# Linear attention ahead of two feed-forward layers: queries and keys of chunks 8 to 23 transposed by 32x32 blocks on VectorE and through DRAM, and query-times-state on 64x64 tiles

## Chip, cores and metric

The kernel runs on one core of a Trainium2 chip. The metric is the device time of one execution in microseconds; before the change the median of three runs is 1184.46 us (1184.09 to 1187.66).

## What is computed

The input is q, k, v of 4 batches x 8 heads x 768 tokens x 64, all float32, and the float64 weights of two feed-forward layers. Attention is a decayed linear recurrence per batch and head, and its output, 3072 tokens x 512, runs through two layers of the same shape:

```python
gamma = 1.0 - 2.0 ** (-5.0 - np.arange(H))
for t in range(S):
    state = gamma * state + outer(k[t], v[t])
    y[t] = (q[t] @ state) / sqrt(D)
x = y.transpose(0, 2, 1, 3).reshape(B * S, H * D)
x = gated(x @ w_in) @ w_out        # h * sigmoid(1.702 h)
out = rational(x @ w2_in) @ w2_out # P(h) / Q(h)
```

## The kernel before

Attention works on 24 chunks of 128 tokens, six per batch. The decays are folded into q and k (`scale_chunk`, line 181): q is multiplied by growing powers of gamma, k by falling ones, on VectorE from chunk 8 on and mostly on GpSimd before. A chunk then has three parts. **T** (`att_T`, lines 198 to 209) transposes q and k with the identity on PE, eight 128x128 transposes into two PSUM banks, and copies them to qT and kT on ACT. **S** (`att_S`, line 211) forms the scores of the eight heads, two heads on the two 64-row halves of PE at a time, and multiplies them by the causal mask on VectorE into sm (line 221). **Y** (`att_Y`, line 224) adds query times state (line 231, called Z below), scores times values (line 234), and, but for the last chunk of a batch, key times value (line 242), which VectorE adds to the state `st` (line 252). `st` holds two heads as diagonal blocks of a 128x128 tile, so the query-times-state matmuls are 128x128 with half of their weights zero; a memset on GpSimd puts the zeros there. y is split into a rounded high part xh (ACT, line 246) and a low part xl (VectorE, line 247).

The layers run in 2 x 6 blocks of 512 tokens and 16 steps each. A step has 12 matmuls of the first product (`g1`, lines 294 to 296, into hp) and 12 of the second (`g2`, lines 313 to 319, into o), each 128x512; between them ACT and VectorE apply the activation (z, gh, gl; lines 367 to 374). `g1` runs two steps ahead in layer 1. VectorE and ACT also turn float64 weight words into float32 (`w_first`, `w_bits`, lines 121 to 136: operations on tiles s and u, here called conversion) and split them into high and low parts (`w_split`, line 147).

Chunks 0 to 3 are done before the first step (the head). Chunks 4 to 23 are spread over the first five blocks of layer 1: a list `todo` (lines 410 to 436) puts the T, S and Y parts of four chunks beside the first 13 steps of each block. All DMAs are issued from SyncE in program order; the other engines' order is set by a scheduler. Raw q, k, v come into a pool of six tiles, so the loads for chunk c+2 wait for chunk c. Scores, transposes and y share two PSUM banks (tag "a"); qT and kT have one buffer each.

Of the kernel before, what the change touches and what calls it, by code (L numbers as in the profile page):

```python
# [9 lines left out]
F32 = mybir.dt.float32  # L10
# [19 lines left out]
def constants():  # L30
    """Identity, causal mask and decay tables: they depend on the shapes alone."""
    gamma = 1.0 - 2.0 ** (-5.0 - np.arange(H, dtype=np.float64))
    t = np.arange(S, dtype=np.float64).reshape(NCH, P)
    up = gamma[None, None, :] ** (t[:, :, None] + 1.0) / np.sqrt(D)
    down = gamma[None, None, :] ** -(t[:, :, None] + 1.0)
    i = np.arange(P)
    c = np.concatenate(
        [
            np.eye(P),
            (i[None, :] >= i[:, None]).astype(np.float64),  # L40
            up.transpose(1, 0, 2).reshape(P, NCH * H),
            down.transpose(1, 0, 2).reshape(P, NCH * H),
        ],
        axis=1,
    )
    return np.ascontiguousarray(c.astype(np.float32))
# [3 lines left out]
def tile_kernel(ctx: ExitStack, tc: tile.TileContext, q, k, v, w1i, w1o, w2i, w2o, pa, pb, cst, out):  # L50
# [27 lines left out]
    # A unit is half of what a step needs: 512 columns of the input or of the output weights.  # L78
    dr_w = {}
# [83 lines left out]

# [1 line left out]
    RAW = {}  # L165
    QK = {}
    SM = {}
    X = {}

    def load_raw(c, nm, pool=None, tag="raw"):  # L170
        b, cc = divmod(c, NCH)
        src = {"q": q, "k": k, "v": v}[nm]
        t = (pool or at).tile([P, H, D], F32, tag=tag, name=f"raw{nm}{c}")
        nc.sync.dma_start(out=t, in_=src[b, :, cc * P : (cc + 1) * P, :].rearrange("h p d -> p h d"))
        RAW.setdefault(c, []).append(t)

# [4 lines left out]
    def scale_chunk(c):  # L181
        cc = c % NCH
        for nm, t in zip("qk", RAW[c]):
            f = tab[nm][:, cc, :].unsqueeze(2).to_broadcast([P, H, D])
            eng = nc.vector if c >= 8 or (c < 4 and nm == "q") else nc.gpsimd
            eng.tensor_tensor(out=t, in0=t, in1=f, op=ALU.mult)
# [10 lines left out]

    def att_T1(c, n, tag, alt=None):
        nm = "qk"[n]
        pt = ps(tag, f"pT{nm}{c}")  # L200
        for p in range(NP):
            nc.tensor.transpose(pt[:, p, :], RAW[c][n][:, 2 * p : 2 * p + 2, :].rearrange("p h d -> p (h d)"), ident)
        t = at_tile(c, nm + "T", alt)
        nc.scalar.copy(out=t, in_=pt)
        QK.setdefault(c, []).append(t)

    def att_T(c, tg, alt=None):
        for n in range(2):
            att_T1(c, n, tg[n], alt)

    def att_S(c, tg, alt=None):
        qT, kT = QK[c]
        pss = [ps(tg[n], f"pS{n}_{c}") for n in range(2)]
        for p in range(NP):
            for n in range(2):
                r = slice(64 * n, 64 * n + 64)
                nc.tensor.matmul(pss[n][:, p, :], kT[r, p, :], qT[r, p, :], start=(p == 0), stop=True, skip_group_check=True)  # L217
        SM[c] = []
        for n in range(2):
            t = at_tile(c, f"sm{n}", alt)  # L220
            nc.vector.tensor_tensor(out=t, in0=pss[n], in1=mask, op=ALU.mult)
            SM[c].append(t)

    def att_Y(c, tg, xh, xl, o):
        b, cc = divmod(c, NCH)
        kr, vr = RAW[c][1:]
        qT = QK[c][0]
# [4 lines left out]
        for p in range(NP):  # L232
            for n in range(2):
                nc.tensor.matmul(  # L234
                    py[64 * n : 64 * n + 64, p, :], vr[:, 2 * p + n, :], SM[c][n][:, p, :],
                    start=(p == 0 and cc == 0), stop=True, skip_group_check=True,
                )
        if cc < NCH - 1:
            pk = ps(tg[1], f"pK{c}")
            for p in range(NP):  # L240
                for n in range(2):
                    nc.tensor.matmul(
                        pk[64 * n : 64 * n + 64, p, 0:D], kr[:, 2 * p + n, :], vr[:, 2 * p + n, :],
                        start=(p == 0), stop=True, skip_group_check=True,
                    )
        nc.scalar.copy(out=xh[:, :, o : o + P], in_=py)
        nc.vector.tensor_tensor(out=xl[:, :, o : o + P], in0=py, in1=xh[:, :, o : o + P].bitcast(F32), op=ALU.subtract)  # L247
        if cc < NCH - 1:
            for n in range(2):
                r = slice(64 * n, 64 * n + 64)  # L250
                if cc:
                    nc.vector.tensor_tensor(out=st[r, :, r], in0=pk[r, :, 0:D], in1=st[r, :, r], op=ALU.add)
                else:
                    nc.vector.tensor_copy(out=st[r, :, r], in_=pk[r, :, 0:D])

# [1 line left out]
    blocks = {1: [4] * 6, 2: [4] * 6}  # L257
    steps = []
# [62 lines left out]
    def evac(layer, bi, t0, n):  # L321
# [11 lines left out]
        for d in range(0, n // P, 2):  # L333
            t = ws.tile([P, 2, DM], F32, tag="s", name=f"os{layer}_{bi}_{d}")
            for x in range(2):
                if last and x:
                    nc.vector.tensor_copy(out=t[:, x, :], in_=acc[d + x])
                else:
                    nc.scalar.copy(out=t[:, x, :], in_=acc[d + x])
                if last:  # L340
                    nc.sync.dma_start(out=out[t0 + (d + x) * P : t0 + (d + x + 1) * P, :], in_=t[:, x, :])
# [66 lines left out]

# [60 lines left out]
    with tc.manual_schedule(engines={mybir.EngineType.SP}):  # L469
# [25 lines left out]
        keep_warm(10)  # L495
        nc.gpsimd.memset(st, 0.0)
        x_tiles(1, 0, blocks[1][0] * P)
# [10 lines left out]

        scale_chunk(0)
        att_T1(0, 0, "a")  # L510
        keep_warm(2)
        att_T1(0, 1, "a")
        keep_warm(2)
        scale_chunk(1)
        att_T1(1, 0, "a", "gh")
        keep_warm(5)
        att_T1(1, 1, "a", "gh")
        S(0)
# [24 lines left out]
        for i in range(-lead[1], NS):  # L543
# [80 lines left out]
```

## Time and profile before

| what | value |
|---|---|
| median of 3 runs | 1184.46 us |
| lowest, highest | 1184.09, 1187.66 us |
| span of the profiled execution (first to last instruction) | 1183.0 us |
| granted TensorE clock, mean of the span | 0.997 |
| PE busy | 1168.6 us, 99% |
| VectorE (DVE) busy | 845.7 us, 71% |
| ScalarE (ACT) busy | 610.4 us, 52% |
| GpSimd (POOL) busy | 15.6 us |

The profiled execution's own time is not listed apart from its span; the runs lie 1.1 to 4.7 us above the span. Busy times are sums over the engine's instructions. Matmuls overlap in the pipeline, so the distance from the start of one to the start of the next tells what it costs, not its own duration.

### The profile page before, as it was taken

The page shows a single profiled execution, that of the slowest core. Times are in us where ns is not written, and L with a number is a line of the kernel's source. Part 1 is how long each engine was busy: PE and PEld are TensorE (multiplying, and loading weights), DVE is VectorE, ACT ScalarE, POOL GpSimd, SP SyncE. Part 2 cuts the span into 40 slices and gives each one's busy share as a digit, 9 for nine tenths or more (in the row PEclk, how much of TensorE's full clock was granted, in tenths as well). Part 3 has the DMA queues.
Part 4 walks back from the last instruction along what each step waited for, and adds up shares of the span by engine and source line. Part 5 has one row for each costly group of instructions (what it writes and reads, how often), then busy time and mean ns, then how long its engine had stood idle before and what let it go on. Part 6 is the DMA issues. An engine that isn't in the chain of part 4 may idle for free.

```text
span 1183.0 us, 15510 instructions
## 1 busy us (share of the span) xinstructions
PE 1168.6 (99%) x6067; PEld 962.7 (81%) x6067; DVE 845.7 (71%) x1372; ACT 610.4 (52%) x1030; POOL 15.6 (1%) x17
## 2 busy tenths in 40 slices
PE   8899999999999999999999999999999999999998
PEld 5787888888888888888888888888888888888887
DVE  6999945545464554553455898888988988988886
ACT  3555523232233323332344876866766766866765
POOL 1100000000000000000000000000000000000000
PEclk9999999999999999999999999999999999999999
DMA  9944233343342423440343200200200200200000
GB/s 255 308 123 114 63 110 88 89 128 86 81 125 77 126 83 101 122 134 1 115 122 109 73 18 1 72 1 1 72 1 1 71 1 1 71 1 1 36 1 36
DMA packets 128600, 89.26 MB, mean 75 GB/s; under 512 B 78224, under 2 KB 111120, under 8 KB 128528
## 3 DMA queue, kind: packets, MB, share of 16 engines
q1 hardware_dynamic: 128528, 88.28, 25.9%
q8 instruction: 47, 0.77, 0.3%
q14 instruction: 25, 0.20, 0.1%
HBM read 67.29 MB, written 20.97 MB: 75 GB/s over the span
## 4 chain that ended last, share of the span: by engine, by line
PE 90%; DVE 8%; issue 1%; DMA 0%; ACT 0%; SPq 0%; POOL 0%
PE hp L294 14%; PE hp L296 14%; PE hp L295 14%; PE o L317 7%; PE o L319 7%; PE o L318 7%; PE o L313 7%; PE o L315 6%; PE o L314 6%; PE pS L217 2%; PE pY L234 2%; DVE u L133 2%; DVE s L135 1%; PE pY L231 1%; DVE s L131 1%; DVE u L132 1%
## 5 line engine op out<-in xcount | busy, mean ns | idle before, releaser
L294 PE MATMUL hp<-xh,wi 128*128 128x512 f32 x768 | 303.4, 395 | 4.9 <-DVE xl L247 2.7
L296 PE MATMUL hp<-xh,wi 128*128 128x512 f32 x768 | 299.7, 390 | 0.0
L295 PE MATMUL hp<-xl,wi 128*128 128x512 f32 x768 | 299.7, 390 | 0.0
L294 PEld LDWEIGHTS hp<-xh,wi 128*128 128x128 f32 x768 | 144.6, 188 | 38.1 <-DVE wi L147 4.5
L296 PEld LDWEIGHTS hp<-xh,wi 128*128 128x128 f32 x768 | 144.6, 188 | 30.7
L295 PEld LDWEIGHTS hp<-xl,wi 128*128 128x128 f32 x768 | 144.6, 188 | 29.0
L367 ACT ACTIVATE z<-hp 128x512 f32<-128x512 f32 x96 | 57.3, 597 | 211.1 <-PE hp L296 210.8
L368 DVE TENSOR_TENSOR z<-hp,z 128x512 f32<-128x512 f32 x96 | 66.1, 688 | 121.8 <-ACT z L367 121.6
L313 PE MATMUL o<-gh,wo 128*128 128x512 f32 x384 | 152.4, 397 | 0.0
L315 PE MATMUL o<-gh,wo 128*128 128x512 f32 x384 | 150.0, 391 | 0.0
L314 PE MATMUL o<-gl,wo 128*128 128x512 f32 x384 | 149.9, 390 | 0.0
L317 PE MATMUL o<-wo,gl 128*128 128x512 f32 x384 | 149.5, 389 | 0.0
L318 PE MATMUL o<-wo,gh 128*128 128x512 f32 x384 | 149.4, 389 | 0.0
L319 PE MATMUL o<-wo,gh 128*128 128x512 f32 x384 | 149.4, 389 | 0.0
L383 ACT ACTIVATE z<-hp 128x512 f32<-128x512 f32 x96 | 57.4, 598 | 145.2 <-PE hp L296 145.2
L386 DVE SCALAR_TENSOR_TENSOR z<-z,ab,w 128x512 f32<-128x512 f32 x96 | 72.0, 750 | 64.0 <-ACT w L384 63.8
L373 ACT CAST gh<-z 128x512 fp32r<-128x512 f32 x96 | 59.8, 623 | 58.8 <-DVE z L368 58.7
L374 DVE TENSOR_TENSOR gl<-z,gh 128x512 fp32r<-128x512 f32 x96 | 66.1, 688 | 29.3 <-ACT gh L373 28.0
L313 PEld LDWEIGHTS o<-gh,wo 128*128 128x128 f32 x384 | 72.1, 188 | 15.9 <-issue 0.2
L315 PEld LDWEIGHTS o<-gh,wo 128*128 128x128 f32 x384 | 72.1, 188 | 15.3
L317 PEld LDWEIGHTS o<-wo,gl 128*128 128x128 f32 x384 | 72.0, 188 | 15.3 <-DVE os L329 0.4
L318 PEld LDWEIGHTS o<-wo,gh 128*128 128x128 f32 x384 | 72.1, 188 | 15.0
(69 smaller groups left out, 1601.7 us busy)
## 6 DMA issues: line engine op xcount, KB each, us to landing
s<-in_moe_w_in_dram SPq DMA_DIRECT2D x32, 512.0 KB, 6.1
s<-in_moe_w_out_dram SPq DMA_DIRECT2D x32, 512.0 KB, 5.9
rawq<-in_q_dram SPq DMA_DIRECT2D x24, 256.0 KB, 4.7
rawk<-in_k_dram SPq DMA_DIRECT2D x24, 256.0 KB, 3.4
rawv<-in_v_dram SPq DMA_DIRECT2D x24, 256.0 KB, 4.0
x2d<-os SPq DMA_DIRECT2D x24, 256.0 KB, 2.1
x<-x2d SPq DMA_DIRECT2D x24, 256.0 KB, 3.0
out_dram<-os SPq DMA_DIRECT2D x10, 512.0 KB, 3.0
```

What stands on the lines that cost most here:

```text
L294: nc.tensor.matmul(hp, wl[:, kk, :], xh[:, kk, :], start=(kk == 0), stop=False)
L295: nc.tensor.matmul(hp, wh[:, kk, :], xl[:, kk, :], start=False, stop=False)
L296: nc.tensor.matmul(hp, wh[:, kk, :], xh[:, kk, :], start=False, stop=(kk == KD - 1))
L313: nc.tensor.matmul(o, wl[:, r], gh, start=a, stop=False)
L314: nc.tensor.matmul(o, wh[:, r], gl, start=False, stop=False)
L315: nc.tensor.matmul(o, wh[:, r], gh, start=False, stop=z)
L317: nc.tensor.matmul(o, gl[:, r], wh, start=a, stop=False)
L318: nc.tensor.matmul(o, gh[:, r], wl, start=False, stop=False)
L319: nc.tensor.matmul(o, gh[:, r], wh, start=False, stop=z)
L368: nc.vector.tensor_tensor(out=z, in0=hp, in1=z, op=ALU.mult)
L374: nc.vector.tensor_tensor(out=gl, in0=z, in1=gh.bitcast(F32), op=ALU.subtract)
L386: nc.vector.scalar_tensor_tensor(out=z, in0=z, scalar=ab[:, 6:7], in1=w, op0=ALU.mult, op1=ALU.add)
```

## The change

For chunks 8 to 23 (`FLAT` is 8) the transposes leave PE. `att_turn` scales q and k of chunk c+1 beside the scores of chunk c, transposes each 32x32 block of the 128x512 tile on VectorE into a tile of the pool `ch` (tag "z", which the activation uses too), and stores it in four DMAs of 32 partitions, in runs of 32 words, so that the DRAM tensor holds the whole transpose. `att_fetch`, in the place of T, loads qT and kT from there. So that two heads lie on the halves of a transposed tile, q and k now pair head p with head p+4: they are loaded in two DMAs each, and the tables are permuted.

For all chunks the state `st` is 128 x 4 x 64 with a head on each 64-row half, without zeros and without the memset. Query times state is eight 64x64 matmuls per chunk in place of four of 128x128. y goes to two PSUM banks, half of each; key times value goes to the other half of the first, and one VectorE operation adds it to the state in place of two. xh and xl are written in two pieces each. The last copy of the output at the end of the kernel is cut in two halves, on ACT and VectorE, with a DMA each.

```diff
-    st = const.tile([P, NP, P], F32, name="st")
+    st = const.tile([P, NP, D], F32, name="st")
...
-        nc.sync.dma_start(out=t, in_=src[b, :, cc * P : (cc + 1) * P, :].rearrange("h p d -> p h d"))
+        if nm == "v":
+            nc.sync.dma_start(out=t, in_=src.rearrange("h t d -> t h d"))
+        else:
+            pairs = t.rearrange("t (p n) d -> t n p d", n=2)
+            for n in range(2):
+                nc.sync.dma_start(out=pairs[:, n], in_=src[NP * n : NP * n + NP].rearrange("p t d -> t p d"))
...
+    def att_turn(c):
+        scale_chunk(c)
+        for nm in "qk":
+            t = ch.tile([P, 2 * H, 32], F32, tag="z", name=f"turn{nm}{c}")
+            nc.vector.transpose(t.rearrange("a x j -> a (x j)"), RAW[c, nm].rearrange("a h d -> a (h d)"))
+            TURN[c, nm] = dr.tile([NP, 2 * D, P], F32, name=f"t{nm}{c}")
+            to = TURN[c, nm].rearrange("p (n h i) (b j) -> b i (p n h) j", n=2, h=2, b=4)
+            for b in range(4):
+                nc.sync.dma_start(out=to[b], in_=t[32 * b : 32 * b + 32])
+
+    def att_fetch(c):
+        for nm in "qk":
+            t = at_tile(c, nm + "T", None)
+            nc.sync.dma_start(out=t, in_=TURN.pop((c, nm)).rearrange("p r t -> r p t"))
+            QK[c, nm] = t
...
     def att_Y(c, tg, xh, xl, o):
-        py = ps(tg[0], f"pY{c}")
+        py = [ps(tg[n], f"pY{n}_{c}") for n in range(2)]
+        pk = py[0].rearrange("a x t -> a (x t)")[:, 2 * P :].rearrange("a (p e) -> a p e", e=D)
         if cc:
             for p in range(NP):
-                nc.tensor.matmul(py[:, p, :], st[:, p, :], qT[:, p, :], start=(p == 0), stop=False, skip_group_check=True)
+                for n in range(2):
+                    r, w = slice(64 * n, 64 * n + 64), slice(64 * (p % 2), 64 * (p % 2) + 64)
+                    nc.tensor.matmul(
+                        py[n][w, p // 2, :], st[r, p, :], qT[r, p, :], start=(p < 2), stop=False, skip_group_check=True
+                    )
...
-        nc.scalar.copy(out=xh[:, :, o : o + P], in_=py)
-        nc.vector.tensor_tensor(out=xl[:, :, o : o + P], in0=py, in1=xh[:, :, o : o + P].bitcast(F32), op=ALU.subtract)
+        for n in range(2):
+            nc.scalar.copy(out=xh[:, 2 * n : 2 * n + 2, o : o + P], in_=py[n][:, 0:2, :])
+        for n in range(2):
+            x = xh[:, 2 * n : 2 * n + 2, o : o + P].bitcast(F32)
+            nc.vector.tensor_tensor(out=xl[:, 2 * n : 2 * n + 2, o : o + P], in0=py[n][:, 0:2, :], in1=x, op=ALU.subtract)
         if cc < NCH - 1:
-            for n in range(2):
-                r = slice(64 * n, 64 * n + 64)
-                if cc:
-                    nc.vector.tensor_tensor(out=st[r, :, r], in0=pk[r, :, 0:D], in1=st[r, :, r], op=ALU.add)
+            if cc:
+                nc.vector.tensor_tensor(out=st, in0=pk, in1=st, op=ALU.add)
...
             if kind == "T":
-                att_T(c, tg)
+                if c < FLAT:
+                    att_T(c, tg)
+                else:
+                    att_fetch(c)
             elif kind == "S":
                 att_S(c, tg)
+                if FLAT <= c + 1 < NT // P:
+                    att_turn(c + 1)
...
                 if c + 2 < NT // P:
                     load_chunk(c + 2)
-                    scale_chunk(c + 2)
+                    if c + 2 < FLAT:
+                        scale_chunk(c + 2)
...
-        nc.gpsimd.memset(st, 0.0)
```

The scheduler orders the instructions of the changed program anew. On PE, in the program before, the scores of chunk 11 (line 217) are followed by 24 weight matmuls and then, here with the last of these, by query times state and scores times values:

```order
L313 MATMUL o_3_1586<-gh_2083,wo_11_1134 128x512
L314 MATMUL o_3_1586<-gl_2084,wo_11_1134 128x512
L315 MATMUL o_3_1586<-gh_2083,wo_11_1134 128x512
L231 MATMUL pY_2200<-qT_2104,st 128x128 x4
L234 MATMUL pY_2200<-sm_11_2155,rawv_1875 64x128
L234 MATMUL pY_2200<-sm_11_2157,rawv_1875 64x128
```

In the changed program the same place on PE, from the last two of chunk 11's eight score matmuls (line 249) to the first of the next step; line 266 is query times state, line 272 scores times values:

```order
L249 MATMUL pS_11_2233<-qT_2197,kT_2199 128x128
L249 MATMUL pS_11_2234<-qT_2197,kT_2199 128x128
L351 MATMUL o_3_1641<-gh_2181,wo_11_1177 128x512
L352 MATMUL o_3_1641<-gl_2182,wo_11_1177 128x512
L353 MATMUL o_3_1641<-gh_2181,wo_11_1177 128x512
L266 MATMUL pY_11_2304<-qT_2197,st 64x128 x4
L272 MATMUL pY_11_2304<-sm_11_2243,rawv_1964 64x128
L266 MATMUL pY_11_2305<-qT_2197,st 64x128 x4
L272 MATMUL pY_11_2304<-sm_11_2243,rawv_1964 64x128 x3
L272 MATMUL pY_11_2305<-sm_11_2245,rawv_1964 64x128 x4
L332 MATMUL hp_2334<-xh_1_745,wi_14_1377 128x512
```

Three weight matmuls stand between the scores and their use where 24 did. On VectorE in the changed program, the masks of chunk 11 (line 253) and what stands ahead of them: a block transpose for chunk 12 (line 231), conversion (lines 136 to 140) and the activation of the step whose hp is 2272 (lines 409 and 415):

```order
L231 STREAM_TRANSPOSE turnk_2256<-rawk_2151 128x512
L136 TENSOR_SCALAR s_5_2163<-s_5_2163 128x512
L409 TENSOR_TENSOR z_2285<-hp_2272,z_2285 128x512
L137 TENSOR_SCALAR u_2366<-u_2366 128x512
L138 SCALAR_TENSOR_TENSOR u_2366<-u_2366,s_5_2163 128x512
L415 TENSOR_TENSOR gl_2289<-z_2285,gh_2288 128x512
L140 SCALAR_TENSOR_TENSOR u_2366<-s_5_2163,u_2366 128x512
L253 TENSOR_TENSOR sm_11_2243<-pS_11_2233,cs 128x512
L253 TENSOR_TENSOR sm_11_2245<-pS_11_2234,cs 128x512
```

The block transposes of the next chunk now stand ahead of this chunk's masks. On SyncE in the changed program, from chunk 10's value load to chunk 11's fetches; tq and tk are the DRAM tensors, w2i, w2o and s weights of layer 2:

```order
L186 DMA rawv_1777<-in_v_dram 128x8x64
L160 DMA w2i<-u_1791 128x4x128
L121 DMA s_2_1798<-in_moe_w_in_dram 128x4x256
L240 DMA qT_1820<-tq_1694 128x4x128
L240 DMA kT_1822<-tk_1701 128x4x128
L235 DMA tq_1874<-turnq_1872 32x16x32 x4
L235 DMA tk_1881<-turnk_1879 32x16x32 x4
L160 DMA w2o<-u_1898 128x512
L123 DMA s_3_1905<-in_moe_w_out_dram 128x1024
L190 DMA rawq_1958<-in_q_dram 128x4x64 x2
```

The fetches stand behind the value load of the chunk after, and the stores of the next chunk behind the fetches.

## Rows read from the trace of the kernel before

**Rows 1.** The page, part 1: span, busy time (share) xinstructions.

```profile
span 1183.0 us, 15510 instructions
...
PE 1168.6 (99%) x6067; PEld 962.7 (81%) x6067; DVE 845.7 (71%) x1372; ACT 610.4 (52%) x1030; POOL 15.6 (1%) x17
```

**Rows 2.** The page, part 4: the chain that ended last, by engine.

```profile
PE 90%; DVE 8%; issue 1%; DMA 0%; ACT 0%; SPq 0%; POOL 0%
```

**Rows 3.** Stretches: us, busy of each engine (instructions), clock, DMA share, GB/s.

```profile
30.00:60.00 30.00, 26.75 (x157) 21.36 (x154) 29.82 (x52) 15.89 (x28) 5.06 (x4) 0.94 1.01 314
...
270.00:376.00 106.00, 106.00 (x635) 87.86 (x635) 55.56 (x96) 31.94 (x54) 0.00 (x0) 1.00 0.35 100
```

**Rows 4.** Timeline of PE around one chunk's transposes: start, duration, what, xcount.

```profile
305.18 0.39 PE L315 MATMUL o<-gh,wo 128*128 128x512 f32 x1
305.41 0.60 PE L202 MATMUL pTq<-cs,rawq 128*128 128x128 f32 x4
...
306.20 0.48 PE L294 MATMUL hp<-xh,wi 128*128 128x512 f32 x1
306.52 0.40 PE L295 MATMUL hp<-xl,wi 128*128 128x512 f32 x1
```

**Rows 5.** Timeline of PE in the Y part of a chunk.

```profile
318.50 1.05 PE L231 MATMUL pY<-qT,st 128*128 128x128 f32 x8
319.48 1.09 PE L234 MATMUL pY<-sm,rawv 128*64 128x128 f32 x16
320.41 0.64 PE L242 MATMUL pK<-rawv,rawk 128*64 128x64 f32 x16
320.97 0.50 PE L294 MATMUL hp<-xh,wi 128*128 128x512 f32 x1
```

**Rows 6.** Timeline of PE and VectorE around a chunk's scores and masks.

```profile
311.51 0.39 PE L315 MATMUL o<-gh,wo 128*128 128x512 f32 x1
311.83 1.16 PE L217 MATMUL pS<-qT,kT 64*128 64x128 f32 x16
312.92 0.50 PE L294 MATMUL hp<-xh,wi 128*128 128x512 f32 x1
...
313.02 1.29 DVE L221 TENSOR_TENSOR sm<-pS,cs 128x512 f32<-128x512 f32 x2 [1.04 <-PE pS L217]
```

**Rows 7.** Groups by line: xcount | busy, mean ns | idle before, releaser.

```profile
L368 DVE TENSOR_TENSOR z<-hp,z 128x512 f32<-128x512 f32 x96 | 66.1, 688 | 121.8 <-ACT z L367 121.6
...
L131 DVE TENSOR_SCALAR s<-s 128x512 int32<-128x512 uint32 x64 | 28.3, 442 | 28.3 <-DMA s<-in_moe_w_out_dram 18.2 <-DMA s<-in_moe_w_in_dram 9.9
...
L252 DVE TENSOR_TENSOR st<-pK,st 64x256 f32<-64x256 f32 x32 | 13.4, 419 | 10.7 <-PE pK L242 10.2
...
L367 ACT ACTIVATE z<-hp 128x512 f32<-128x512 f32 x96 | 57.3, 597 | 211.1 <-PE hp L296 210.8
```

**Rows 8.** DMA queues, 305 to 311 us, one query load: packets, MB, share.

```profile
q1 hardware_dynamic: 1040, 0.26, 19.2%
```

**Rows 9.** DMA queues, 600 to 604 us, two reloads, mostly 512 B packets.

```profile
q1 hardware_dynamic: 610, 0.40, 32.7%
```

**Rows 10.** DMA queues, 270 to 376 us, four chunks.

```profile
q1 hardware_dynamic: 18432, 10.49, 35.0%
```

**Rows 11.** Timeline of SyncE's queue after a chunk's end on PE.

```profile
321.50 0.57 SPq L174 DMA_DIRECT2D rawv<-in_v_dram  x1
...
323.22 0.38 SPq L118 DMA_DIRECT2D s<-in_moe_w_out_dram  x1
323.70 0.41 SPq L155 DMA_DIRECT2D w2i<-u  x1
```

**Rows 12.** The page, part 6: xcount, KB each, median us from issue to landing.

```profile
s<-in_moe_w_in_dram SPq DMA_DIRECT2D x32, 512.0 KB, 6.1
```

**Rows 13.** Timeline around the first g1 matmul.

```profile
35.85 0.68 DVE L247 TENSOR_TENSOR xl<-pY,xh 128x512 fp32r<-128x512 f32 x1
...
36.59 0.79 PE L294 MATMUL hp<-xh,wi 128*128 128x512 f32 x1 [2.73 <-DVE xl L247]
```

More of the change, by code (lines that the diff above doesn't have):

```diff
@@ L36, in constants, with flat @@
     i = np.arange(P)
+    def flat(f):
+        return f.reshape(NCH, P, 2, NP).transpose(1, 0, 3, 2).reshape(P, NCH * H)
     c = np.concatenate(
@@ L40, in constants @@
             (i[None, :] >= i[:, None]).astype(np.float64),
-            up.transpose(1, 0, 2).reshape(P, NCH * H),
-            down.transpose(1, 0, 2).reshape(P, NCH * H),
+            flat(up),
+            flat(down),
         ],
@@ L162, in w_reload @@
         STG[u] = m
+    blocks = {1: [4] * 6, 2: [4] * 6}
     RAW = {}
+    TURN = {}
     QK = {}
@@ L181, in scale_chunk @@
     def scale_chunk(c):
[L182 to L185, printed above, removed]
+        for nm in "qk":
+            t = RAW[c, nm]
+            f = tab[nm][:, c % NCH, :].unsqueeze(2).to_broadcast([P, H, D])
+            eng = nc.vector if c >= FLAT or (c < 4 and nm == "q") else nc.gpsimd
             eng.tensor_tensor(out=t, in0=t, in1=f, op=ALU.mult)
@@ L224, in att_Y @@
     def att_Y(c, tg, xh, xl, o):
-        b, cc = divmod(c, NCH)
-        kr, vr = RAW[c][1:]
-        qT = QK[c][0]
-        py = ps(tg[0], f"pY{c}")
+        cc = c % NCH
+        kr, vr = RAW.pop((c, "k")), RAW.pop((c, "v"))
+        qT = QK.pop((c, "q"))
+        py = [ps(tg[n], f"pY{n}_{c}") for n in range(2)]
+        pk = py[0].rearrange("a x t -> a (x t)")[:, 2 * P :].rearrange("a (p e) -> a p e", e=D)
         if cc:
             for p in range(NP):
-                nc.tensor.matmul(py[:, p, :], st[:, p, :], qT[:, p, :], start=(p == 0), stop=False, skip_group_check=True)
-        for p in range(NP):
-            for n in range(2):
+                for n in range(2):
[4 more added lines that the diff above has]
+        for n in range(2):
+            for p in range(NP):
+                w = slice(64 * (p % 2), 64 * (p % 2) + 64)
                 nc.tensor.matmul(
-                    py[64 * n : 64 * n + 64, p, :], vr[:, 2 * p + n, :], SM[c][n][:, p, :],
-                    start=(p == 0 and cc == 0), stop=True, skip_group_check=True,
+                    py[n][w, p // 2, :], vr[:, NP * n + p, :], SM[c][n][:, p, :],
+                    start=(p < 2 and cc == 0), stop=True, skip_group_check=True,
                 )
+        del SM[c]
         if cc < NCH - 1:
-            pk = ps(tg[1], f"pK{c}")
             for p in range(NP):
@@ L242, in att_Y @@
                     nc.tensor.matmul(
-                        pk[64 * n : 64 * n + 64, p, 0:D], kr[:, 2 * p + n, :], vr[:, 2 * p + n, :],
-                        start=(p == 0), stop=True, skip_group_check=True,
-                    )
-        nc.scalar.copy(out=xh[:, :, o : o + P], in_=py)
-        nc.vector.tensor_tensor(out=xl[:, :, o : o + P], in0=py, in1=xh[:, :, o : o + P].bitcast(F32), op=ALU.subtract)
-        if cc < NCH - 1:
-            for n in range(2):
-                r = slice(64 * n, 64 * n + 64)
-                if cc:
-                    nc.vector.tensor_tensor(out=st[r, :, r], in0=pk[r, :, 0:D], in1=st[r, :, r], op=ALU.add)
-                else:
-                    nc.vector.tensor_copy(out=st[r, :, r], in_=pk[r, :, 0:D])
-    blocks = {1: [4] * 6, 2: [4] * 6}
+                        pk[64 * n : 64 * n + 64, p, :], kr[:, 2 * p + n, :], vr[:, NP * n + p, :],
+                        start=False, stop=True, skip_group_check=True,
+                    )
+        for n in range(2):
+            nc.scalar.copy(out=xh[:, 2 * n : 2 * n + 2, o : o + P], in_=py[n][:, 0:2, :])
+        for n in range(2):
+            x = xh[:, 2 * n : 2 * n + 2, o : o + P].bitcast(F32)
+            nc.vector.tensor_tensor(out=xl[:, 2 * n : 2 * n + 2, o : o + P], in0=py[n][:, 0:2, :], in1=x, op=ALU.subtract)
+        if cc < NCH - 1:
+            if cc:
+                nc.vector.tensor_tensor(out=st, in0=pk, in1=st, op=ALU.add)
+            else:
+                nc.vector.tensor_copy(out=st, in_=pk)
     steps = []
@@ L335, in evac @@
             for x in range(2):
[L336 to L341, printed above, removed]
+                cut = 2 if last and d + x == len(acc) - 1 else 1
+                for y in range(cut):
+                    m = slice(y * DM // cut, (y + 1) * DM // cut)
+                    if last and (x if cut == 1 else y):
+                        nc.vector.tensor_copy(out=t[:, x, m], in_=acc[d + x][:, m])
+                    else:
+                        nc.scalar.copy(out=t[:, x, m], in_=acc[d + x][:, m])
+                    if last:
+                        nc.sync.dma_start(out=out[t0 + (d + x) * P : t0 + (d + x + 1) * P, m], in_=t[:, x, m])
             if not last:
@@ L509, in tile_kernel @@
         scale_chunk(0)
-        att_T1(0, 0, "a")
+        att_T1(0, "q", "a")
         keep_warm(2)
-        att_T1(0, 1, "a")
+        att_T1(0, "k", "a")
         keep_warm(2)
         scale_chunk(1)
-        att_T1(1, 0, "a", "gh")
+        att_T1(1, "q", "a", "gh")
         keep_warm(5)
-        att_T1(1, 1, "a", "gh")
+        att_T1(1, "k", "a", "gh")
         S(0)
```

19 lines of the change are left out of this document (11 added, 8 removed).

## The prediction

> **What bounds the kernel now.** I read the busy times first: PE is busy 1168.6 of 1183.0 us, no other engine above 71% [rows 1]. The chain of waits agrees: 90% of it is PE [rows 2]. So the question for each edit is what it takes from PE's stream or puts into it, and whether something it leans on arrives too late. The stretches tell where the change lands: chunks 8 to 23 run from about 180 to 580 us, and in the stretch 270 to 376 PE has no idle time while VectorE is busy 55.56 of 106 us. Only the head differs: between 30 and 60 us VectorE is busy 29.82 of 30 us [rows 3]. The runs lie at 1184.09 to 1187.66 us with a median of 1184.46; the profiled span is 1.5 us below that median, which I carry as what lies around it. A change under 0.3% (3.6 us) can't be told from none.
>
> **Transposes gone from PE.** In a dense stretch one 128x512 matmul starts 0.23 us after another: 305.18 to 305.41. The eight transposes of a chunk begin at 305.41, and the second matmul behind them starts at 306.52, where without them it would start at 305.41 + 0.23 = 305.64 [rows 4]. A chunk pays 0.88 us. 16 chunks lose them: **-14.1 us**. The order of the change shows no transpose on PE from chunk 8 on, so this doesn't hang on anything hidden.
>
> **Query times state (Z).** Now 8 instructions per chunk (each matmul runs as two) take from 318.50 to 319.48, 0.98 us, or 0.122 us each; there is no change of tile shape ahead of them [rows 5]. Then there are 16, on 64x64 tiles, entered by a change of shape. Entering the 64-row tiles of the scores costs 311.83 - 311.51 - 0.23 = 0.09 us [rows 6]. The pace of 64x64 tiles is not in the trace. Bounds: the 16 of the key-value products take 320.97 - 320.41 = 0.56 us, 0.035 each; the 16 of the scores, two row halves at a time, 312.92 - 311.83 = 1.09 us, 0.068 each; the 16 of line 234, two column halves, 0.93 us [rows 5, 6]. I take 0.040, nearest to the key-value row, because its weights are also 64 columns wide and four tiles may run where the other two rows have two: 16 x 0.040 + 0.09 = 0.73 us, a gain of 0.25. The ends are a gain of 0.33 and a loss of 0.20. The Trainium skill (TensorEngine Tiling (Array Packing), Tiling Modes) calls 64x64 four independent tiles; by it, as an estimate, Z would take half of 0.98, a gain of about 0.4, which no row here shows.
> Of the 20 chunks with a state, three lie in the head, where PE isn't the limit. Four (4, 11, 15, 19) are written as four matmuls to one bank, one other, four to the second bank: only one row half at a time, so line 234's 0.93 us, plus 0.09 to enter and two more changes of shape at about 0.1: +0.24 each. 13 x 0.25 - 4 x 0.24 = **-2.3 us**, ends -4.3 + 1.0 = -3.3 and +2.6 + 1.0 = +3.6.
>
> **What hides the new way.** VectorE gets two 128x512 transposes per chunk. No row has one; the nearest are 0.69 us (line 368) and, for the shorter, 0.44 us (line 131); twice the longer is the upper end. Against that the state update shrinks from two 64x256 operations of 0.42 us to one, and the low half of y splits into two pieces of about 0.42 in place of one of the size of line 368 [rows 7]. Net 0.6 to 2.5 us, about 1.1, per chunk of some 26 us, in which VectorE is idle for nearly half: nothing, while that cover stands. ACT loses two copies per chunk and gains none.
> The DMA engines: 1040 packets of mostly 256 B held 16 engines for 19.2% of 6 us, 17.7 ns a packet [rows 8]. A chunk's turned blocks leave in 4096 runs of 128 B: between 9 (by bytes) and 17.7 ns (by packets), I take the upper: 4096 x 17.7 / 16 = 4.5 us of all engines. The fetch is 1024 runs of 512 B at 0.327 x 4 x 16 / 610 = 34 ns: 2.2 us [rows 9]. The load now is 35.0% of 106 us for four chunks, 9.3 us each [rows 10]; with 6.7 more it is 16 us of some 26. SyncE gets eight stores, two loads and two fetches per chunk, at 0.4 to 0.6 us [rows 11]: about 6 us of its queue, mostly idle.
> Then the path. Fetches stand behind the loads of the chunk after next, whose value load waits for the previous chunk's end on PE. From that load's issue at 321.50 three issues take until 323.22 + 0.38, two fetches in the form of 323.70 take 0.9 more [rows 11]: 3 us. They land 4 to 6 us later, since loads and a 512 KB weight piece, which alone takes 6.1, are ahead [rows 12]. On PE 63 to 76 weight matmuls, 14.3 to 17.2 us, stand between the end of one chunk and the scores of the next (48 before the last chunk, which has no loads ahead). About 5 us are left: nothing. The order puts the turned blocks of chunk c+1 ahead of chunk c's masks, so the stores have begun by then.
>
> **The masks.** This is where cover shrinks. Scores to the first use of the masks was 24 weight matmuls (5.4 us) on PE; the order of the change has, in chunks 8 to 23, 3 (three times), 4, 9 (three times), 13, 15, 17 (twice) and 23 or 24 (five times). And the first Z matmul now writes a bank that the scores held, so it too waits for a mask. The two masks end 313.02 + 1.29 = 314.31, 1.4 us after the scores [rows 6], if VectorE is free. For chunk 11 it isn't: z of step hp_2272 stands ahead of the masks. PE runs 9 matmuls (2.0), the scores (1.2 with entry) and 3 matmuls (0.8): Z's turn comes 4.0 us after hp_2272 ends. The other side needs 0.6 on ACT (line 367), then on VectorE z, two conversion operations, gl, another conversion and the first mask, 0.69 each but for one of 0.44 [rows 7]: 4.5 us. Stall 0.5 and 0.2 for the second mask. Three such chunks at 0.7 and 0.2 for chunk 13: **+2.3 us**; ends 0 and the rival below.
>
> **Head and end.** VectorE sets the first g1: the low half of chunk 3's y starts at 35.85 and hp starts at 36.59 [rows 13]. The order of the change puts five more conversion operations ahead of that piece (0.42 to 0.7 each, 2.9 us), four more halves (0.6), and takes three state pieces (1.26) away: 2.2 us later. The converted weights are done earlier, which may give some back, and q and k loads come in halves: **+1.5 us**, ends -1 and +3. At the end the last copy, a 128x512 piece like line 368, becomes two halves of about 0.42 on two engines, with one more DMA issue: **-0.2 us**, ends -0.4 and 0.2.
>
> **Sum:** -14.1 - 2.3 + 2.3 + 1.5 - 0.2 = -12.8. The span goes from 1183.0 to 1170.2, the time to 1184.46 - 12.8 = **1171.7 us**. With the terms' ends it reaches 1165 to 1180.
>
> **Rivals.**
> *VectorE late for the masks* (0.12). The same order, but VectorE one conversion behind: 0.44 + 0.44 + 0.69 + 0.69 = 2.2 us, as where it waits for a weight piece (28.3 us in all ahead of line 131 [rows 7]). Eleven chunks have under 18 matmuls of cover; if nine of them lose 2 us, that is +18 in place of 2.3: 1187 us, no change. For it: order on VectorE is fixed. Against: half idle.
> *The stores are slow* (0.07). If a 128 B write costs far more than a 256 B read, the stores land after the fetch is due. With 4.5 us of engine time the fetch has about 5.5 us to spare, 5.5 x 16 / 4096 = 21 ns a packet: the point is 39 ns. At three times the row, 53 ns, each of 15 chunks stalls PE by 256 x 14 ns = 3.6 us: +54, so 1226 us, **slower**. For it: no run here writes to DRAM in pieces this short. The Trainium skill (DMA: Bandwidth & Descriptors, Specifications) says that transfers below 512 B are done as read-modify-write; that is the rule by which this would happen. Against: the 256 B reads run at 17.7 ns.
> *64x64 tiles run one after the other* (0.04): 16 x 0.122 + 0.09 = 2.05 us, 1.07 more in 17 chunks, +18.2 in place of -2.3: 1192 us. Against: both kinds of halves in rows 5 and 6 overlap.
>
> **Numbers.** Forecast 0.75, the rest 0.02 unnamed. Faster: the forecast nearly whole (0.74) and a third of the first rival: 0.78. Same: most of the rest of that rival: 0.09. Slower: 0.13. The range takes the forecast's ends and the milder half of the first rival: 1164 to 1184.
>
> **What would show it.** Right: no transpose rows from chunk 8; 128x512 matmuls following each other directly there; Z about 0.6 us; PE waiting on masks for 1 to 5 us in all; the stores landing within 6 us. Wrong: PE waiting for qT or kT by DMA, masks above 10 us, a first hp after 40 us, or Z above 1 us.

## The result, and the profile after

The changed kernel takes 1173.16 us (median of 4 runs, 1171.79 to 1176.27); the kernel before took 1185.14 us beside it (4 runs, 1184.09 to 1187.66). The ratio is 0.9901, 95% interval 0.9878 to 0.9924: 12 us, or 1%, faster, where 12.8 us were forecast. The execution that was profiled is the slowest of the four, 1176.27 us, so its span is only 8.5 us below that of before. Its page, part 1, and its chain of waits by engine:

```profile
span 1174.5 us, 15951 instructions
...
PE 1153.2 (98%) x6099; PEld 943.2 (80%) x6099; DVE 855.2 (73%) x1408; ACT 593.0 (50%) x1023; POOL 19.5 (2%) x16
...
PE 89%; DVE 7%; DMA 2%; issue 1%; ACT 1%; SPq 1%; POOL 0%; DVEq 0%; ACTq 0%
```

PE has 15.4 us less to do than in [rows 1], and DMA now has a place in the chain. The stretches (busy us of each engine, then granted clock, DMA share, GB/s):

```profile
20.00:34.00 14.00, 10.38 (x90) 8.61 (x90) 9.42 (x19) 5.78 (x11) 1.92 (x2) 0.50 0.99 269
...
30.00:60.00 30.00, 26.39 (x202) 21.21 (x201) 26.52 (x50) 16.34 (x32) 4.89 (x4) 0.86 1.05 321
270.00:376.00 106.00, 105.28 (x641) 85.60 (x638) 61.22 (x109) 29.19 (x52) 0.00 (x0) 1.00 0.59 145
```

Against [rows 3], the dense stretch 270 to 376 has gained VectorE work (61.22 in place of 55.56) and DMA share (0.59 in place of 0.35), and PE now has 0.7 us of idle time there; in the head the clock is lower, at 0.50 (1.2 GHz) from 20 to 34 us. The timeline of PE, at the place of [rows 4], in a dense chunk as [rows 5], and in chunk 15, where query times state is split:

```profile
305.19 0.39 PE L351 MATMUL o<-gh,wo 128*128 128x512 f32 x1
305.42 0.39 PE L352 MATMUL o<-gl,wo 128*128 128x512 f32 x1
305.64 0.39 PE L353 MATMUL o<-gh,wo 128*128 128x512 f32 x1
...
317.84 0.39 PE L353 MATMUL o<-gh,wo 128*128 128x512 f32 x1
318.16 0.67 PE L266 MATMUL pY<-qT,st 64*64 64x128 f32 x16
318.76 1.09 PE L272 MATMUL pY<-sm,rawv 128*64 128x128 f32 x16
319.68 0.64 PE L280 MATMUL pY<-rawv,rawk 128*64 128x64 f32 x16
320.25 0.50 PE L332 MATMUL hp<-xh,wi 128*128 128x512 f32 x1
320.58 0.39 PE L333 MATMUL hp<-xl,wi 128*128 128x512 f32 x1
...
339.02 0.65 PE L266 MATMUL pY<-qT,st 64*64 64x128 f32 x8
339.60 0.43 PE L272 MATMUL pY<-sm,rawv 128*64 128x128 f32 x2
339.97 0.65 PE L266 MATMUL pY<-qT,st 64*64 64x128 f32 x8
340.55 0.98 PE L272 MATMUL pY<-sm,rawv 128*64 128x128 f32 x13
341.26 0.28 PE L280 MATMUL pY<-rawv,rawk 128*64 128x64 f32 x2
341.37 0.27 PE L272 MATMUL pY<-sm,rawv 128*64 128x128 f32 x1
341.38 0.72 PE L280 MATMUL pY<-rawv,rawk 128*64 128x64 f32 x14
342.03 0.50 PE L333 MATMUL hp<-xl,wi 128*128 128x512 f32 x1
342.37 0.40 PE L334 MATMUL hp<-xh,wi 128*128 128x512 f32 x1
```

Read the starts. Weight matmuls follow each other at 0.23 us where the transposes stood. A query times state whose products stand together (called dense) takes 318.76 - 318.16 = 0.60 us; in chunk 15 products of line 272 stand between its halves (called split). From its start to the second weight matmul behind the chunk it is 320.58 - 318.16 = 2.42 us when dense and 342.37 - 339.02 = 3.35 when split: 0.93 more. What PE waited for (us in all, times, longest):

```profile
PE pS L249 <- DMA kT<-tk: 3.0, 3, 1.9
PE pY L266 <- DVE st L293: 2.9, 1, 2.9
PE pY L272 <- DVE sm L253: 2.0, 1, 2.0
...
PE hp L332 <- DVE xl L288: 1.7, 1, 1.7
PE pTq L217 <- DVE rawq L202: 1.6, 1, 1.6
...
PE pY L266 <- DVE sm L253: 0.5, 2, 0.3
```

The first row is new, and of the new waits it is the one outside the head that costs: it stands ahead of chunks 8, 12 and 16, each the first of a block. The timeline of the third place, chunk 16:

```profile
365.67 1.77 SPq L368 DMA_DIRECT2D x2d<-os  x2
...
366.51 0.58 ACT L365 COPY os<-o 128x512 f32<-128x512 f32 x1
...
367.49 0.43 SPq L240 DMA_DIRECT2D qT<-tq  x1
367.97 0.90 SPq L240 DMA_DIRECT2D kT<-tk  x1
...
370.97 0.39 PE L334 MATMUL hp<-xh,wi 128*128 128x512 f32 x1
...
372.08 1.16 PE L249 MATMUL pS<-qT,kT 64*128 64x128 f32 x16 [0.72 <-DMA kT<-tk]
```

SyncE issues the fetches right behind the stores that end a block, and the last of those stores waits for ACT's copy of the accumulator at 366.51. The fetch of kT, issued at 367.97, lets the scores start at 372.08, 4.1 us later; PE was ready for them at 370.97 + 0.39 = 371.36, 3.4 us after the issue.

The stores themselves are quick. The DMA queues from 288 to 292 us, when nothing but turned blocks was moved (packets, MB, share; then the issues):

```profile
DMA packets 2674, 0.33 MB, mean 83 GB/s; under 512 B 2674, under 2 KB 2674, under 8 KB 2674
...
q1 hardware_dynamic: 2674, 0.33, 52.6%
...
tk<-turnk SPq DMA_DIRECT2D x4, 64.0 KB, 2.0
```

That is 0.526 x 4 us x 16 / 2674 = 12.6 ns a packet. VectorE's new groups by line (busy, mean ns, idle before):

```profile
L288 DVE TENSOR_TENSOR xl<-pY,xh 128x256 fp32r<-128x256 f32 x48 | 19.1, 421 | 14.4 <-ACT xh L285 14.0
...
L231 DVE STREAM_TRANSPOSE turnq<-rawq 128x512 f32<-128x512 f32 x16 | 11.3, 707 | 0.0
```

### The profile page after: what moved, and what is told of

Read it like the earlier page. It is cut to its first block, busy times and chain, and to the rows that moved or that the text cites. A ratio compares the mean times of both kernels' runs of the same rounds, so it can differ in the third digit from the quotient of the medians.

```text
span 1174.5 us, 15951 instructions
## 1 busy us (share of the span) xinstructions
PE 1153.2 (98%) x6099; PEld 943.2 (80%) x6099; DVE 855.2 (73%) x1408; ACT 593.0 (50%) x1023; POOL 19.5 (2%) x16
## 4 chain that ended last, share of the span: by engine, by line
PE 89%; DVE 7%; DMA 2%; issue 1%; ACT 1%; SPq 1%; POOL 0%; DVEq 0%; ACTq 0%
PE hp L332 14%; PE hp L333 14%; PE hp L334 14%; PE o L355 7%; PE o L357 7%; PE o L356 7%; PE o L351 6%; PE o L352 6%; PE o L353 6%; PE pS L249 2%; PE pY L272 2%; DVE u L138 1%; DVE s L140 1%; DMA kT<-tk 1%; PE pY L266 1%
## 5 line engine op out<-in xcount | busy, mean ns | idle before, releaser
L355 PEld LDWEIGHTS o<-wo,gl 128*128 128x128 f32 x384 | 72.0, 188 | 15.4 <-DVE os L367 0.4
```

The costliest lines, as they stand in the source:

```text
L355: nc.tensor.matmul(o, gl[:, r], wh, start=a, stop=False)
```

## The experiments

Where the time lies is read in four pieces in every kernel: when the first product of the feed-forward starts, from there to step 16, from step 16 to step 80 (the stretch in which chunks 8 to 23 run), then the rest. From step 80 to the last step the profiled executions of before and of the change take the same, so the three first columns are what differs (us; each from one profiled execution, starts of the hp matmuls; the median is of all runs):

| kernel | first product | step 0 to 16 | step 16 to 80 | median | ratio to before (95%) |
|---|---|---|---|---|---|
| before | 36.59 | 106.06 | 421.45 | 1185.14 | |
| changed | 41.21 | 103.96 | 410.38 | 1173.16 | 0.9901 (0.9878 to 0.9924) |
| changed, again | 38.59 | 103.33 | 409.05 | 1171.83 | 0.9890 (0.9874 to 0.9907) |
| transposes on PE again | 38.74 | 104.97 | 418.32 | 1183.07 | 0.9989 (0.9980 to 0.9998) |
| transposes alone | 36.41 | 103.88 | 409.33 | 1172.23 | 0.9898 (0.9884 to 0.9911) |
| early fetch | 36.59 | 103.33 | 404.17 | 1166.18 | 0.9854 (0.9839 to 0.9869) |
| zeros in the head | 35.11 | 104.86 | 409.13 | 1169.61 | 0.9881 (0.9867 to 0.9894) |
| early fetch and zeros | 35.58 | 104.73 | 403.84 | 1165.57 | 0.9843 (0.9830 to 0.9857) |
| the same, from chunk 6 | 36.54 | 103.34 | 403.86 | 1166.51 | 0.9849 (0.9832 to 0.9866) |
| early fetch, state in halves | 39.88 | 102.81 | 404.09 | 1167.54 | 0.9862 (0.9848 to 0.9875) |
| early fetch, stores twice | 38.20 | 104.00 | 448.03 | 1206.90 | 1.0189 (1.0176 to 1.0203) |
| early fetch, turned twice | 39.93 | 102.80 | 408.41 | 1173.72 | 0.9909 (0.9896 to 0.9923) |

**Transposes on PE again.**

```diff
-    FLAT = 2 * blocks[1][0]
+    FLAT = NT // P
...
-            eng = nc.vector if c >= FLAT or (c < 4 and nm == "q") else nc.gpsimd
+            eng = nc.vector if c >= 8 or (c < 4 and nm == "q") else nc.gpsimd
```

> The changed kernel with one part undone: chunks 8 to 23 are transposed on PE again; the new query-times-state, the halved loads and the cut last copy stay. Theory (the transposes are what the change gains, and their new way costs only the wait of three fetches): 16 x 0.88 = 14.1 us come back and the 3.0 us that PE waits for kT go, so about 11 us above the changed kernel, 1184 us, level with the kernel before. Rival (the gain comes as much from the smaller query-times-state and the masks' order as from the transposes): at most 7 us above the changed kernel, 1180 or less.

The time went back to 1183.07 us, 9.9 above the changed kernel: the transposes carry the gain, and the rival falls. The sum came out 1 us short because PE's order changed too: in this kernel query times state is whole in every chunk from 8 on. Steps 16 to 80 take 7.94 us more than in the changed kernel: +14.1, less the 3.0 of the fetches, less three split chunks at 0.93, less about 0.3 of chunk 13 (split unevenly), is 8.0.

**Transposes alone**, in the kernel before, with `att_turn` and `att_fetch` as in the change; the diff shows where they are called.

```diff
...
-                att_T(c, tg)
+                if c < 8:
+                    att_T(c, tg)
+                else:
+                    att_fetch(c)
...
                 att_S(c, tg)
+                if 8 <= c + 1 < NT // P:
+                    att_turn(c + 1)
...
-                    scale_chunk(c + 2)
+                    if c + 2 < 8:
+                        scale_chunk(c + 2)
```

> The kernel before with one part of the change alone: queries and keys of chunks 8 to 23 are turned on VectorE and go through DRAM; the state stays block-diagonal and query-times-state runs on 128x128 tiles. Theory: -14.1 for the transposes, +3.0 for the late fetches, masks between 0 and +2.3: the profiled span 1173 to 1175 and the time 1173 to 1176, a little above the changed kernel but for the head, which stays that of the kernel before (first product of the feed-forward at 36 to 37 us). Rival (the new query-times-state is needed for the gain, since it frees the bank and takes the wait off the masks): above 1178 us.

1172.23 us, level with the changed kernel and 0.8 us below the range that I gave, so the rival falls here too: everything else in the change, as it is ordered there, is worth nothing that the medians show. One number of mine was wrong: PE waited for kT only 0.2 us:

```profile
PE pS L235 <- DMA kT<-tk: 0.2, 1, 0.2
```

Whether the fetch at a block's start is late depends, it seems, on when the copies of the accumulators get their turn; no run varies that alone.

**Early fetch.**

```diff
-                else:
-                    att_fetch(c)
...
                 att_Y(c, tg, *X[1, bi], o)
+                if FLAT <= c + 1 < NT // P:
+                    att_fetch(c + 1)
                 if c + 2 < NT // P:
```

> The changed kernel with one thing moved: the two fetches of a chunk are issued right behind the chunk before it, ahead of the loads of raw chunks and of the four x2d stores that end a block. Theory (at a block's start the fetch stands on SyncE behind those four stores, which wait for copies of the accumulators, 362.47 to 367.44 in the changed kernel): the three waits for kT, 3.0 us in all, go to 0 and the time falls by about 3 us, to 1169 to 1170. Rival (the way through DRAM itself is too slow, stores and fetch share full DMA engines): the waits for kT stay at 2 us or more, the time stays within 1 us of the changed kernel's.

The waits for kT are gone, and the way through DRAM is not too slow. But the time fell by about twice what I expected, to 1166.18 us: 7.0 below the changed kernel's first median and 5.7 below its second. Steps 16 to 80 lost 6.2 us: the 3.0 of the fetches, and 3.1 because the scheduler, given another place for the fetch, no longer splits query times state in chunks 11, 13, 15 and 19 (three at 0.93 and about 0.3). PE is never idle in the dense stretch of this kernel:

```profile
270.00:376.00 106.00, 106.00 (x661) 86.30 (x661) 59.03 (x105) 27.58 (x50) 0.00 (x0) 1.00 0.59 143
```

**Zeros in the head, and the changed kernel again.** The first has two more groups of products of zeros:

```diff
         Y(0)
+        wt = ps("a", "wt1").rearrange("p a b -> p (a b)")
+        keep_warm(14)
...
         S(2)
+        wt = ps("a", "wt2").rearrange("p a b -> p (a b)")
+        keep_warm(8)
```

> The changed kernel with 22 more products of zeros on PE in the head, 14 behind chunk 0 and 8 around the scores of chunk 2, where PE sat idle for 2.9, 1.6, 0.9 and 2.0 us; nothing else moves. Theory (the head is 4.6 us longer because PE ran at half clock from 18.1 to 35.2 us in the profiled run, where the kernel before did so only from 16.1 to 19.5): the granted clock stays full through the head, the first product of the feed-forward comes at 37 to 38 us in place of 41.2, and the time falls to 1169 to 1171 with less spread between runs. Rival (VectorE's order sets the head, as the prediction has it): the first product stays at 40 us or later and the time within 1 us of the changed kernel's.

> The changed kernel once more, nothing altered, for the head: its instructions stand on PE and VectorE in the same order as in the early fetch for the first 190 of each, and yet the first product of the feed-forward came at 41.21 us there and at 36.59 with the early fetch. Theory (the head's length changes from run to run with the stretches at half clock): the median stays at 1172 to 1174.5, the runs spread over 3 us or more, and the first product comes at a time that goes with the length of the half-clock stretches, 20 us of them for 41.2 and 7 us for 36.6. Rival (the changed kernel's head is longer by its order): the first product at 41 us again, whatever the clock, and a spread under 2 us.

The stretch 0 to 36.5 us of the changed kernel, of its second profile, of the early fetch, whose head has the same order, and of the kernel with zeros (clock: third number from the end):

```profile
0.00:36.50 36.50, 26.73 (x243) 19.81 (x243) 20.99 (x39) 13.34 (x26) 7.52 (x10) 0.77 0.99 242
```

```profile
0.00:36.50 36.50, 26.59 (x261) 19.61 (x263) 21.60 (x42) 14.06 (x26) 7.21 (x10) 0.81 0.97 236
```

```profile
0.00:36.50 36.50, 26.72 (x291) 19.57 (x291) 22.84 (x47) 14.78 (x29) 6.52 (x10) 0.91 1.00 244
```

```profile
0.00:36.50 36.50, 29.02 (x314) 18.83 (x314) 24.81 (x48) 14.94 (x29) 6.46 (x10) 1.00 1.00 243
```

At a mean clock of 0.77 the first product starts at 41.21 us, at 0.81 at 38.59, at 0.91 at 36.59, at 1.00 at 35.11; the kernel before had 0.95 and 36.59. The first three have one order of instructions. So the head's 4.6 us in the profiled run went with the clock and not with the order of the change, and with the zeros they are gone: 1169.61 us, with a first product 1.5 us earlier than in the kernel before. The zeros did not act on the clock alone, though: in that kernel the transposes of chunk 2 stand between the products of chunk 1's query times state (at 18.87 and 19.83 us, among products from 16.84 to 20.42), so something else moved after all. Nor does the head go with the clock alone (two other kernels with the same head, stores twice and turned twice, had 38.20 and 39.93 at 0.86), and why the clock fell further in one run than in another of the same order stays open. And the spread that I expected of the changed kernel's runs did not come back: 1171.50 to 1172.22 this time.

**Both together.** The edits of the early fetch and of the zeros.

> The early fetch and the 22 products of zeros in the head together. Theory (the two act in different stretches: the fetch and the order of the split chunks between 100 and 580 us, the clock in the head): the gains over the changed kernel add, so 1163 to 1165 us and a first product of the feed-forward at 35 to 36 us, with a spread of at most 2 us between runs. Rival (the early fetch's run had a good head by chance and its median already holds the gain): 1166 us or more, as with the early fetch alone.

1165.57 us, between the two expectations, and not to be told from the early fetch alone. In the profiled runs its first product comes 1.0 us earlier, but steps 0 to 16 take 1.4 us longer, so nothing of it is left at step 16; the early fetch's profiled head was already a good one.

**State in halves**, on top of the early fetch.

```diff
-            for p in range(NP):
-                for n in range(2):
+            for n in range(2):
+                for p in range(NP):
                     r, w = slice(64 * n, 64 * n + 64), slice(64 * (p % 2), 64 * (p % 2) + 64)
```

> The early fetch, with query-times-state written as four products to one bank, then four to the other, in every chunk, so that only two of the four 64x64 tiles can run beside each other. Theory (four tiles run at once, and a split chunk is slow because it uses two): its 16 instructions take 1.16 us in place of 0.60, as the halves of the split chunks with 8 in 0.58, so 17 chunks with 0.56 more each: about +9 us over the early fetch, 1175 us. Rival (an instruction on a 64x64 tile costs 0.0375 us whatever runs beside it, and a split chunk is slow by its two changes of tile shape alone): 0.60 us stays and the time stays within 1 us of the early fetch's.

The theory falls. The timeline of PE in a dense chunk:

```profile
311.58 0.39 PE L353 MATMUL o<-gh,wo 128*128 128x512 f32 x1
311.90 0.68 PE L266 MATMUL pY<-qT,st 64*64 64x128 f32 x16
312.51 1.09 PE L272 MATMUL pY<-sm,rawv 128*64 128x128 f32 x16
```

0.61 us, as before the edit; steps 16 to 80 are the same too (404.09 and 404.17), and the 1.4 us more of the median, which the rival did not expect either, lie ahead of them: the profiled head is 3.3 us longer. The order in which the sixteen are issued doesn't matter. Yet in a split chunk eight of them alone take 0.58 us, nearly as long as sixteen, so the rival's fixed price per instruction falls too. That fits PE starting a later instruction on a free tile ahead of an earlier one whose tile is busy; for these sixteen it is argued, not shown.

**Turned twice, and stores twice**, both on top of the early fetch.

```diff
-            nc.vector.transpose(t.rearrange("a x j -> a (x j)"), RAW[c, nm].rearrange("a h d -> a (h d)"))
+            for _ in range(2):
+                nc.vector.transpose(t.rearrange("a x j -> a (x j)"), RAW[c, nm].rearrange("a h d -> a (h d)"))
```

```diff
+            more = dr.tile([NP, 2 * D, P], F32, name=f"m{nm}{c}").rearrange("p (n h i) (b j) -> b i (p n h) j", n=2, h=2, b=4)
+            for b in range(4):
+                nc.sync.dma_start(out=more[b], in_=t[32 * b : 32 * b + 32])
```

> The early fetch, with each of the 32 transposes on VectorE issued twice: 0.70 us more for each of queries and keys, 1.4 us per chunk. PE's order changes with it: chunks 15, 19 and 23 have query-times-state split, +2.3 us by itself at 0.77 each. Theory (VectorE has room): the waits for masks stay below 2 us outside the head and the time is 1168 to 1169 us. Rival (VectorE late for the masks, as the prediction's first rival): the waits for masks grow by 8 us or more, 1174 us or more.

> The early fetch, with each turned block also stored a second time, to another place in DRAM that nobody reads: 4096 more runs of 128 B per chunk and eight more issues on SyncE. PE's order changes with it: 13 of the chunks from 8 on have query-times-state split, which by the changed kernel's split chunks (0.77 us more each) is +10 us by itself. Theory (the way through DRAM is hidden with room for as much again): PE never waits over 0.5 us in all for qT or kT, and the time is 1174 to 1177 us, all of it from the order. Rival (the stores are near the limit): PE waits for qT or kT by 5 us or more in all, above 1180 us.

Turned twice took 1173.72 us, almost 5 us above my range and near the rival's number, but not by the rival's way: PE waited for masks 0.2 us outside the head. 4.2 us lie in steps 16 to 80: 2.8 by three split chunks at 0.93 (I had 0.77), 0.8 by chunk 12's scores, which the new order puts in three pieces, and 0.5 by an accumulator copied late. Another 3.3 lie in a long head. VectorE's room for the transposes is real, as far as the masks go.

Stores twice took 1206.9 us, and neither theory holds. PE did not wait for qT or kT at all, so the stores are not what ended late. It waited for other things (us, times, longest):

```profile
PE o L354 <- DVE os L370: 13.0, 3, 5.0
PE pY L269 <- DVE sm L256: 9.2, 13, 0.8
```

The timeline of the longest of them:

```profile
273.05 1.16 PE L252 MATMUL pS<-qT,kT 64*128 64x128 f32 x16
...
274.25 1.29 DVE L256 TENSOR_TENSOR sm<-pS,cs 128x512 f32<-128x512 f32 x2 [4.01 <-PE pS L252]
...
276.05 0.70 DVE L231 STREAM_TRANSPOSE turnq<-rawq 128x512 f32<-128x512 f32 x1
276.68 0.67 DVE L231 STREAM_TRANSPOSE turnk<-rawk 128x512 f32<-128x512 f32 x1
...
278.53 0.58 ACT L368 COPY os<-o 128x512 f32<-128x512 f32 x1
...
281.35 0.68 DVE L370 COPY os<-o 128x512 f32<-128x512 f32 x1
...
282.09 0.80 PE L354 MATMUL o<-gh,wo 128*128 128x512 f32 x1 [4.97 <-DVE os L370]
```

The scheduler's new order puts the copy that frees an accumulator behind masks which wait 4.01 us for PE, and behind transposes and conversion, and PE waits for the copy. In 12 chunks it also puts the first product that needs a mask right behind the scores, with nothing between to hide the mask. Of the 13 split chunks that I had counted, 11 are broken by products of line 272; chunks 16 and 20 have their halves behind each other with nothing between, as in the kernel with state in halves, which costs next to nothing. 13.0 + 9.2 + 11 x 0.93 = 32.4 of the 43.9 us in steps 16 to 80. Another 5.4 us are no loss: 24 more weight matmuls stand ahead of step 80's first, and the steps behind it take 5.0 us less. Behind each of the three idle stretches the clock was granted at half for some time (0.50 from 282 to 288 us); some 35 matmuls started 0.43 us apart there in place of 0.23, which by estimate is 7 us and covers the rest. What the doubled stores cost by themselves stays open: the edit moved too much else.

**From chunk 6**, on top of both together.

```diff
-    FLAT = 2 * blocks[1][0]
+    FLAT = 6
```

> The early fetch and the zeros in the head, with chunks 6 and 7 turned on VectorE too. There VectorE is not half idle: between 42 and 145 us of the changed kernel it is busy 98.20 of 103 us, with the conversion of weights that PE needs next. Each of the two chunks takes 0.88 us from PE and puts two transposes (0.70 each) and two scalings (0.69 each, until now on GpSimd) on VectorE, 2.8 us. Theory (the change pays only where VectorE has room): 5.6 us more against 4.8 us idle, so weights come later, PE waits longer for wi, and the time is 1165 to 1169 us, not below the early fetch with the zeros, 1165.6. Rival (idle time of VectorE doesn't matter, the transposes are free anywhere): 2 x 0.88 less, 1163.8 us.

1166.51 us, no gain, as the theory has it; but its reason is not seen. The profiled run waited for wi less than the one without the edit (0.6 us, in place of 1.0), and steps 0 to 16 took 103.3 us in place of 104.7, 1.4 us less where the two chunks' transposes are worth 1.8. In these steps PE waited 1.1 us for a piece of the activation (gh), which it didn't without the edit, and chunk 7 is split now; the first product came 1.0 us later. The difference of the medians lies within both spreads. So this run can't tell the two apart.

## Why the prediction was right, point by point

**Transposes, -14.1: right.** No transpose stands on PE from chunk 8, and the weight matmuls close up to 0.23 us. Both one-part experiments agree. One reading beside it was off: in the kernel before, chunks 8 to 23 run from 139 to 553 us, not from about 180 to 580; no term rests on that.

**Query times state, -2.3: right in sign, and mis-sized.** The dense chunk gains 0.98 - 0.60 - 0.09 (the entry, 318.16 - 317.84 - 0.23) = 0.29 us, where 0.25 was forecast. The kernel with the transposes on PE again bears that out, since its 14 chunks with a state from 8 on are all dense: its steps 16 to 80 take 421.45 + 0.88 - 418.32 = 4.0 us less, 0.29 each (the 0.88 because chunk 8's transposes stand ahead of step 16 in the kernel before and behind it there). The Trainium skill's rule of four independent tiles (TensorEngine Tiling (Array Packing), Tiling Modes) gave half of 0.98 for the products and a gain of 0.4 as an estimate; the trace agrees in part, with 0.60 for the products and a gain of 0.29. Split chunks were under-priced: 0.93 over a dense chunk is 0.64 over before, in place of 0.24, since a split breaks the products of line 272 too: one of the eight matmuls, two instructions, stands between the halves at 339.60, and the other seven behind them, each part with its own entry. With four split chunks and 12 dense ones, and chunk 13 about even, the term is -3.5 + 2.6 = -0.9.

**What hides the new way, 0: the step that failed.** VectorE's part is hidden: a transpose takes 0.70 us, as taken from line 368, and doubling them left the masks alone. The DMA engines' part is hidden too: 12.6 ns a store packet against the 17.7 taken, 2.0 us to landing against 6 allowed, and a DMA share of 0.59 of 106 us for four chunks, 15.6 us each against 16. What failed is "about 5 us are left: nothing", the wait for the fetch that was put at 0. I took the slack of a chunk in the middle of a block, where the fetch stands behind loads. At a block's start it stands on SyncE behind four stores of the block's result, and these wait for the accumulators' copies. There the slack on PE looked longest and the queue was latest: 3.0 us (1.4 in the second profile), and none once the fetch was issued ahead of those stores.

**The masks, +2.3: too much.** Outside the head the waits for masks are the 0.5 us of line 266, twice. Of the three chunks priced at 0.7 only chunk 11 waited, 0.3 us.

**Head, +1.5: the cause was another.** VectorE's order, from which I worked it out, costs nothing that can be seen: the same order gave 36.59 us with the early fetch, as before. The first product moved by +4.6 us in the profiled run and +2.0 in the second, with the half-clock stretch. What came ahead of it is 2.9 us in which PE waited for the state's copy at line 293, which in the new order stands behind both halves of xl; but the early fetch has the same wait and a head as short as before, so the wait alone does not explain it. Some 2 us came back by step 16, as the prediction allowed: the two kernels are 4.6 us apart at the first product and 2.5 at step 16 (142.65 and 145.17), and about 0.9 of the difference is chunk 8's transposes.

**End, -0.2: nothing.** From the start of the last matmul to the end it is 4.1 us before and 4.2 after. The second half's copy on VectorE waited 1.07 us for ACT's copy of the first, so the halves did not run beside each other.

The forecast time was met in part by luck, because errors cancel: the masks cost 2 us less, the fetches 1.4 to 3.0 more, and state and head together 2 to 4.5 more, less what came back by step 16. The terms as measured add up for the profiled run: -14.1 for the transposes, -0.9 for the state, +3.0 for the fetches, +4.6 for the head, -1.2 for what else came back by step 16, -8.6 in all against 8.5 us less span.

**The rivals.** VectorE late for masks: not seen, even with doubled transposes. Stores slow: not seen; a 128 B packet took 12.6 ns, far from the 39 at which it would have decided. The Trainium skill's rule that transfers under 512 B are done as read-modify-write (DMA: Bandwidth & Descriptors, Specifications) can't be told from the ordinary price of a small packet here: 12.6 ns lies between the 9 by bytes and the 17.7 by packets of the prediction. Tiles one after the other: not seen.

## What to carry to other kernels

Work that leaves the bounding engine by way of DRAM has two due times: when its transfer is quick enough, and when its queue lets it be issued. Look for the slack at the place where the queue is latest (behind a store that waits for compute), not at a typical chunk; two issues moved ahead of those stores took 3.0 us of waits away. And where a scheduler orders the program, a change of one DMA moves matmuls too: the same move kept four chunks from being split, worth another 3.1 us, and storing the blocks twice cost 41 us without one wait for qT or kT. Compare the order before a difference is put down to the transfer.

## What the runs showed of the hardware

Sixteen instructions on four 64x64 tiles take 0.60 us, and eight that use two of the tiles between two changes of tile shape take 0.58. In chunk 15 of the changed program all products of line 272 stand ahead of the key-value products of line 280, and yet by the rows above a group of two of the latter starts at 341.26, ahead of the last of line 272 at 341.37. The Trainium skill (TensorE: Matmul & The Clock Gate, Part 3: Packing small matmuls — row/col tiling) has matmuls start strictly in program order; these records disagree. In the head the clock's fall cost more than the instructions that the change added there: with one order, the first product came at 41.21 us at a mean clock of 0.77 and at 36.59 at 0.91; with 22 products of zeros, in an order that moved a little, at 35.11 at 1.00.
